# A spectral block with an MLP: evicting an item ahead of the casts of the one before

## The chip, the cores and the metric

The kernel runs on one core of a Trainium2 chip. The core has a matrix engine (TensorE, PE), a vector engine (VectorE, DVE), a scalar engine (ScalarE, ACT), a general one (GpSimd, POOL) and a queue for transfers (SyncE, SP). Each works through its own list of instructions in order and waits for the others by semaphores. Matmuls write into PSUM, here eight banks of 128 partitions x 512 float32. The metric is the device time of one launch in microseconds.

## The reference

```python
mod = (silu(c) @ w_mod).reshape(1, 6, 1, 512)        # sa, ca, ga, sb, cb, gb
h = layernorm(x) * (1 + ca) + sa                     # x: 2048 x 512
x = x + ga * irfft2(rfft2(h) * (w_r + 1j * w_i))
h = layernorm(x) * (1 + cb) + sb
x = x + gb * (mish(h @ w1 + b1) @ w2)                # w1: 512 x 1376, w2: 1376 x 512
```

The first half is a spectral filter, the second an MLP with a Mish between its two matrix products. The change concerns the MLP alone.

## The kernel before

The filter comes first and takes the first 150 us or so; its last steps overlap the first steps of the MLP. All matrix products of the MLP are made in fp32r with the operands split: `split` writes a rounded copy (the high part, a cast on ScalarE) and the remainder (the low part, a subtraction on VectorE), and three products of parts (`TERMS`) stand for one.

**Blocks and items.** The 2048 rows are worked in `NB` = 8 blocks of 256. For each block the 1376 hidden features are worked in `NT` = 6 items: item 0 has the last 96 features, items 1 to 5 have two tiles of 128. Step s of the loop (`mlp`, 48 in all) is item s % 6 of block s // 6. A step has

- `up`: TensorE multiplies w1 with the block's normalised input `h2`, one PSUM bank for a tile (tags A and D, two banks each);
- `mish`: for each tile ScalarE copies half of the bank with the bias added (L731) and VectorE adds the other half (L732); ScalarE applies the Mish (L734); VectorE makes four sums of the quarters (L744), which the multiplication of 2 x 2 blocks with seven products (Strassen's, in Winograd's form) needs;
- `high` and `low`: the casts (L754) and the remainders (L760) of the seven quarters and sums, the `acts` of the item;
- `down` of the item two steps earlier (`LAG` = 2): seven products of three matmuls each, added up in four banks (tags B and C, `out_ps`) over the block. Item 0 has six plain matmuls instead.

The w2 of an item is loaded (`load_w2`), its sums are made on GpSimd (`sum_w2`), and it is split in two parts (`split_w2`: raw and sums). Items 4 and 5 get theirs while block 0 runs.

**The next block's input.** In step 3 `norm_pair` normalises the next 256 rows on ScalarE (L141). In steps 4 and 5 `transpose_in` transposes half of the columns each, into a bank of tag A, then of tag D; `split_in` scales them (L624) and splits them into `h2` (L628, L629). `up` of the next block's item 0 reads all of `h2`.

**The result of a block.** In step 1 of the next block, after `down` of the last item, `gather` copies two banks and `chain` adds up the four results (L801 to L805). After the remainders of that step, `residual` finishes the sums, multiplies with the gate gb (L812), adds to x (L814) and stores.

**The last block.** Its items 4 and 5 are multiplied in the plain way (`down_last`: w2 unsplit into sums, loaded again by `load_w2`, split by `plain_w2`), so that most of the result can be added up before the last products; `finish` multiplies by the gate and stores the two halves one after the other.

The order on each engine is the order in which the program writes the instructions (`manual_schedule`); tile pools give buffers in rotation, and an instruction that takes a buffer waits for the last reader of its earlier content.

Of the kernel before, what the change touches and what calls it, by code (L numbers as in the profile page):

```python
# [30 lines left out]
def tile_spectral_block(ctx: ExitStack, tc: tile.TileContext, x_d, w1_d, b1_d, w2_d,  # L31
# [620 lines left out]
    def w2_space(t):  # L652
# [6 lines left out]
        if t == 4:  # L659
# [27 lines left out]
    def split_w2(t, sums):  # L687
# [23 lines left out]
    tsum = modr[:, 0:2].rearrange("p r (e d) -> p (r e) d", d=256)  # L711

    def up(g):
        b, t = divmod(g, NT)
        h = h2[b]
        ups[g] = []
        for e, f, rows in tiles(t):
            ps = bank("CD"[e] if g < 2 else "AD"[e])[:rows]
            fs = slice(f * P, f * P + rows)
            for k in range(4):  # L720
                nc.tensor.matmul(ps, w1h[:, k, fs], h[:, k], start=(k == 0), stop=False)  # L721
            for k in range(4):
                nc.tensor.matmul(ps[:, 0:256], w1l[:, k, fs], h[:, k, 0], start=False, stop=(k == 3))  # L723
            ups[g].append((e, f, ps))

    def mish(g):
        w = buf("g1")
        for e, f, ps in ups.pop(g):
            rows = ps.shape[0]
            o = w[:rows, 256 * e:256 * e + 256]  # L730
            nc.scalar.activation(o, ps[:, 256:], AF.Identity, bias=b1n[:rows, f:f + 1])  # L731
            nc.vector.tensor_tensor(o, o, ps[:, 0:256], op=ALU.add)  # L732
        o = w[:rows, 0:256 * e + 256]
        nc.scalar.activation(o, o, AF.Mish)  # L734
        parts = [(o, slice(0, 2))]
        if g >= total - 2:
            parts = [(w, slice(0, 4))]
        elif g % NT:
            u = buf("g2")
            a = w.rearrange("p (e s) -> p e s", s=P)  # L740
            v = u.rearrange("p (e s) -> p e s", s=P)
            for o, p, q, op in ((v[:, 0], a[:, 0], a[:, 2], ALU.add), (v[:, 1], v[:, 0], a[:, 1], ALU.subtract),
                                (v[:, 2], a[:, 1], a[:, 0], ALU.subtract), (v[:, 3], a[:, 3], v[:, 1], ALU.subtract)):
                nc.vector.tensor_tensor(o, p, q, op=op)  # L744
            parts = [(w[:, P:], slice(0, 3)), (u, slice(3, 7))]
        return parts

    def high(g, parts):
        hi, lo = acts[g] = [act.tile([P, 7, P], F32R, name=n) for n in ("ah", "al")]
        flat = []  # L750
        for r, c in parts:
            n = r.shape[0]
            h, l = (z[:n, c].rearrange("p e s -> p (e s)") for z in (hi, lo))
            nc.scalar.copy(h, r)  # L754
            flat.append((l, r, plain(h)))
        return flat

    def low(parts):
        for l, r, h in parts:
            nc.vector.tensor_tensor(l, r, h, op=ALU.subtract)  # L760

    def down(g):
        b, t = divmod(g, NT)
        a = acts.pop(g)
        if t == 0:
            out_ps[b] = out = [bank(n) for n in "CBBC"]
# [4 lines left out]
        out = out_ps[b]  # L771
        for n, half, e, r in END if g == total - 3 else RAW + SUM:
            o = out[n][:, 256 * half:256 * half + 256]
            own = n in (0, 3)
            last = t == 5 or (own and g == total - 3)
            for i, (p, q) in enumerate(TERMS):
                nc.tensor.matmul(o, a[p][:, e], w2[t][q][:, r], start=(own and half == 0 and t == 1 and i == 0),  # L777
                                 stop=(last and i == 2 and (n, half) != (1, 0)), skip_group_check=own)

    def down_last():  # L780
        out = out_ps[NB - 1]
        for n, half in ((2, 0), (1, 1)):
            for g in (total - 2, total - 1):
                for f in range(2):
                    for i, (p, q) in enumerate(TERMS):
                        nc.tensor.matmul(out[n], acts[g][p][:, half + 2 * f],
                                         w2["plain", g % NT][q][:, 512 * f:512 * f + 512],
                                         start=False, stop=(g == total - 1 and f == 1 and i == 2))

    rows = modr[:, 0:2]  # L790

# [7 lines left out]
    def chain(b):  # L799
        p, q = done[b]  # L800
        nc.vector.tensor_tensor(rows[:, 1], out_ps[b][1], p, op=ALU.add)  # L801
        nc.vector.tensor_tensor(q[:, 0:256], q[:, 0:256], p[:, 0:256], op=ALU.add)
        nc.vector.tensor_tensor(q[:, 256:], q[:, 256:], q[:, 0:256], op=ALU.add)
        both = q[:, 256:].unsqueeze(1).to_broadcast([P, 2, 256])
        nc.vector.tensor_tensor(rows[:, 0].rearrange("p (j d) -> p j d", j=2),  # L805
                                out_ps[b][2].rearrange("p (j d) -> p j d", j=2), both, op=ALU.add)

    def residual(b):
        p, q = done.pop(b)
        nc.vector.tensor_tensor(rows[:, 1, 256:], rows[:, 1, 256:], q[:, 0:256], op=ALU.add)  # L810
        nc.vector.tensor_tensor(rows[:, 0, 256:], rows[:, 0, 256:], p[:, 256:], op=ALU.add)
        nc.vector.tensor_tensor(rows, rows, gbr.unsqueeze(1).to_broadcast([P, 2, D]), op=ALU.mult)  # L812
        xb = x[:, 2 * b:2 * b + 2, :]
        nc.vector.tensor_tensor(xb, xb, rows, op=ALU.add)  # L814
        nc.sync.dma_start(ov[:, 2 * b:2 * b + 2, :], xb)

    total = NB * NT
    ctx.enter_context(tc.manual_schedule())

    def mlp(s):  # L820
        b, t = divmod(s, NT)
        nxt = 2 * b + 2 if b < NB - 1 else None
        up(s)
        if t in (4, 5) and nxt:
            transpose_in(nxt, t - 4)
        if t == 3 and nxt:
            norm_pair(nxt)
# [12 lines left out]
        if t == 1 and b:  # L840
            residual(b - 1)

    def finish():
        b = NB - 1
        p, q = buf("h"), buf("h")
        nc.scalar.copy(p, out_ps[b][0])
        nc.scalar.copy(q, out_ps[b][3])
        u, v = rows[:, 1], rows[:, 0]
        nc.scalar.copy(u[:, 0:256], p[:, 0:256])
        nc.vector.tensor_tensor(q[:, 0:256], q[:, 0:256], p[:, 0:256], op=ALU.add)  # L850
        nc.vector.tensor_tensor(u[:, 256:], q[:, 0:256], p[:, 256:], op=ALU.add)  # L851
        nc.vector.tensor_tensor(v[:, 0:256], q[:, 256:], q[:, 0:256], op=ALU.add)
        nc.vector.tensor_tensor(v[:, 256:], v[:, 0:256], p[:, 256:], op=ALU.add)
        nc.gpsimd.tensor_tensor(u, u, gbr, op=ALU.mult)  # L854
        down_last()
        xu, xv = x[:, 2 * b + 1, :], x[:, 2 * b, :]
        nc.vector.tensor_tensor(v, out_ps[b][2], v, op=ALU.add)
        nc.vector.tensor_tensor(v, v, gbr, op=ALU.mult)
        nc.vector.tensor_tensor(xv, xv, v, op=ALU.add)
        nc.sync.dma_start(ov[:, 2 * b:2 * b + 1, :], x[:, 2 * b:2 * b + 1, :])  # L860
        nc.gpsimd.tensor_tensor(xu, xu, u, op=ALU.add)
        nc.vector.tensor_tensor(q, out_ps[b][1], gbr, op=ALU.mult)
        nc.vector.tensor_tensor(xu, xu, q, op=ALU.add)
        nc.sync.dma_start(ov[:, 2 * b + 1:2 * b + 2, :], x[:, 2 * b + 1:2 * b + 2, :])

    apply_gate()
    prep = {s: [] for s in range(N2 + 1)}
# [32 lines left out]
        if s in (7, 8):  # L900
            split_in(0, s - 7)
    norm_scale(N2 - 4, N2)
    low(high(0, mish(0)))
    split_w2(0, False)
    low(high(1, mish(1)))
    load_w2(4)
    sum_w2(4, 0, 1, 2, 3)
    for s in range(LAG, total):
        mlp(s)
        if s == 3:  # L910
            split_w2(4, False)
            split_w2(4, True)
            load_w2(5)
            sum_w2(5, 0, 1, 2, 3)
        if s == 5:
            split_w2(5, False)
            split_w2(5, True)
        if s == total - 4:
            load_w2(4)
        if s == total - 3:  # L920
            plain_w2(4)
            load_w2(5)
        if s == total - 2:
            plain_w2(5)
    finish()


def _constants():
# [133 lines left out]
```

## Time and profile before

| | us |
|---|---|
| median of three runs | 427.79 (426.19 to 429.06) |
| the profiled execution | 427.04 |
| its span | 425.23 |
| six blocks, from the input's wait of block 1 to that of block 7 | 196.01 |
| from there to the end of the span | 42.1 |

The span is the time from the first to the last instruction of the profiled execution. The profile has a busy time for each engine, a chain of waits, and a timeline; TensorE's rows give the start of a matmul and its modelled end, so that in a dense stretch the distance of two starts is what a matmul costs, and a row in square brackets names what the engine waited for.

### The profile page before, as it was taken

The page shows a single profiled execution, that of the slowest core. Times are in us where ns is not written, and L with a number is a line of the kernel's source. Part 1 is how long each engine was busy: PE and PEld are TensorE (multiplying, and loading weights), DVE is VectorE, ACT ScalarE, POOL GpSimd, SP SyncE. Part 2 cuts the span into 40 slices and gives each one's busy share as a digit, 9 for nine tenths or more (in the row PEclk, how much of TensorE's full clock was granted, in tenths as well). Part 3 has the DMA queues.
Part 4 walks back from the last instruction along what each step waited for, and adds up shares of the span by engine and source line. Part 5 has one row for each costly group of instructions (what it writes and reads, how often), then busy time and mean ns, then how long its engine had stood idle before and what let it go on. Part 6 is the DMA issues. An engine that isn't in the chain of part 4 may idle for free.

```text
span 425.2 us, 7487 instructions
## 1 busy us (share of the span) xinstructions
PE 394.4 (93%) x2791; PEld 360.6 (85%) x2791; DVE 300.6 (71%) x654; ACT 253.3 (60%) x546; POOL 91.1 (21%) x127
## 2 busy tenths in 40 slices
PE   8999899999999999689989989989989989999994
PEld 8888788899899998588879979979979979888883
DVE  2999959676189986786766765775774774764866
ACT  2777755577459646774674674575475484475371
POOL 0677526565067521110000000000000000000002
PEclk9999999999999999899999999999999999999999
DMA  8999852281223411100100100100100100100211
GB/s 290 350 359 356 252 200 76 81 321 47 76 83 100 134 43 27 51 2 0 51 0 2 49 2 0 52 0 2 52 0 2 49 2 0 51 2 2 99 51 49
DMA packets 20180, 35.73 MB, mean 84 GB/s; under 512 B 3632, under 2 KB 6480, under 8 KB 19760
## 3 DMA queue, kind: packets, MB, share of 16 engines
q1 hardware_dynamic: 19712, 34.73, 24.0%
q10 hardware_dynamic: 432, 0.53, 0.3%
q8 instruction: 22, 0.36, 0.3%
q14 instruction: 14, 0.11, 0.1%
HBM read 31.06 MB, written 4.19 MB: 83 GB/s over the span
## 4 chain that ended last, share of the span: by engine, by line
DVE 40%; PE 25%; ACT 19%; issue 6%; DMA 5%; POOL 3%; SPq 0%; POOLq 0%; DVEq 0%; ACTq 0%
PE bank L721 6%; DVE buf L744 6%; DVE buf L732 5%; ACT buf L734 5%; DVE al L760 5%; PE bank L777 4%; DMA buf<-in_B_w_dram 4%; PE bank L723 3%; DVE st L112 3%; PE bank L456 3%; PE bank L502 3%; ACT ah L754 3%; ACT buf L141 2%; DVE ve L125 2%; ACT buf L624 2%
## 5 line engine op out<-in xcount | busy, mean ns | idle before, releaser
L760 DVE TENSOR_TENSOR al<-buf,ah 128x512 fp32r<-128x512 f32 (+2 forms) x86 | 50.1, 603 | 20.6 <-ACT ah L754 20.6
L734 ACT ACTIVATE buf<-buf 128x512 f32<-128x512 f32 (+1 forms) x48 | 28.6, 597 | 53.4 <-DVE buf L732 53.4
L744 DVE TENSOR_TENSOR buf<-buf 128x128 f32<-128x128 f32 x152 | 39.8, 303 | 28.2 <-ACT buf L734 25.8
L721 PE MATMUL bank<-h2e,w1h 128*128 128x512 f32 (+1 forms) x176 | 50.6, 407 | 8.7 <-DVE h2e L629 4.4
L754 ACT CAST ah<-buf 128x512 fp32r<-128x512 f32 (+2 forms) x86 | 45.5, 552 | 18.2 <-DVE buf L744 11.0
L721 PE MATMUL bank<-h2o,w1h 128*128 128x512 f32 (+1 forms) x176 | 49.5, 399 | 6.9 <-DVE h2o L629 5.6
L731 ACT ACTIVATE buf<-bank,b1n 128x256 f32<-128x256 f32 (+1 forms) x88 | 38.5, 467 | 28.2 <-PE bank L723 28.2
L732 DVE TENSOR_TENSOR buf<-buf,bank 128x256 f32<-128x256 f32 (+1 forms) x88 | 34.0, 416 | 26.2 <-ACT buf L731 26.2
L854 POOL TENSOR_TENSOR modr<-modr 128x512 f32<-128x512 f32 x1 | 1.3, 1343 | 234.6 <-DVE modr L851 234.6
L721 PEld LDWEIGHTS bank<-h2e,w1h 128*128 128x128 f32 (+1 forms) x176 | 30.5, 191 | 15.1 <-DVE h2e L629 5.8
L721 PEld LDWEIGHTS bank<-h2o,w1h 128*128 128x128 f32 (+1 forms) x176 | 29.8, 187 | 13.2 <-DVE h2o L629 7.4
L777 PE MATMUL bank<-w2a,ah 128*128 128x256 f32 x168 | 36.8, 285 | 0.0
L777 PE MATMUL bank<-w2b,ah 128*128 128x256 f32 x147 | 31.8, 283 | 0.0
L723 PEld LDWEIGHTS bank<-h2e,w1l 128*128 128x128 f32 (+1 forms) x176 | 27.2, 189 | 4.2
L723 PEld LDWEIGHTS bank<-h2o,w1l 128*128 128x128 f32 (+1 forms) x176 | 26.7, 185 | 4.1
L723 PE MATMUL bank<-h2e,w1l 128*128 128x256 f32 (+1 forms) x176 | 28.2, 283 | 0.0
L777 PEld LDWEIGHTS bank<-w2a,ah 128*128 128x128 f32 x168 | 28.0, 191 | 0.0
L723 PE MATMUL bank<-h2o,w1l 128*128 128x256 f32 (+1 forms) x176 | 27.8, 280 | 0.0
L234 PE MATMUL bank<-buf,mring 128*128 128x512 f32 x48 | 21.4, 446 | 4.2 <-DVE buf L227 1.9
L637 PE MATMUL bank<-kc,d 128*128 128x128 f32 x128 | 24.9, 276 | 0.5 <-ACT d L360 0.5
L112 DVE BATCH_NORM_STATS2 st<-x 128x6 f32<-128x512 f32 x32 | 22.0, 688 | 4.3 <-DMA x<-in_A_x_dram 3.9
L638 PE MATMUL bank<-kc,d 128*128 128x128 f32 x128 | 24.7, 275 | 0.0
(216 smaller groups left out, 1015.5 us busy)
## 6 DMA issues: line engine op xcount, KB each, us to landing
buf<-in_B_w_dram SPq DMA_DIRECT2D x22, 256.0 KB, 2.7
xring<-in_x_t_dram SPq DMA_DIRECT2D x16, 256.0 KB, 4.7
x<-in_A_x_dram SPq DMA_DIRECT2D x16, 256.0 KB, 5.0
wm<-in_w_mod_dram SPq DMA_DIRECT2D x16, 256.0 KB, 4.3
out_dram<-x SPq DMA_DIRECT2D x7, 512.0 KB, 2.6
mraw<-in_km_dram SPq DMA_DIRECT2D x16, 128.0 KB, 4.8
wqa<-in_w_q_dram SPq DMA_DIRECT2D x8, 256.0 KB, 4.3
wqb<-in_w_q_dram SPq DMA_DIRECT2D x8, 256.0 KB, 4.7
```

Of the source, the lines that this page charges most:

```text
L112: nc.vector.bn_stats(t, x[:, n, :])
L637: nc.tensor.matmul(o, dj[:, 0:128], kc[0][:, n, :], start=True, stop=False)
L638: nc.tensor.matmul(o, dj[:, 64:192], kc[1][:, n, :], start=False, stop=True)
L721: nc.tensor.matmul(ps, w1h[:, k, fs], h[:, k], start=(k == 0), stop=False)
L723: nc.tensor.matmul(ps[:, 0:256], w1l[:, k, fs], h[:, k, 0], start=False, stop=(k == 3))
L731: nc.scalar.activation(o, ps[:, 256:], AF.Identity, bias=b1n[:rows, f:f + 1])
L732: nc.vector.tensor_tensor(o, o, ps[:, 0:256], op=ALU.add)
L734: nc.scalar.activation(o, o, AF.Mish)
L744: nc.vector.tensor_tensor(o, p, q, op=op)
L754: nc.scalar.copy(h, r)
L760: nc.vector.tensor_tensor(l, r, h, op=ALU.subtract)
L777: nc.tensor.matmul(o, a[p][:, e], w2[t][q][:, r], start=(own and half == 0 and t == 1 and i == 0), stop=(last and i == 2 and (n, half) != ...
```

## The change

- The step is put together anew. `front` (bias and add) of item s comes first, then the casts and remainders of item s - 1 (`halves`, cast and remainder of each part in turn), then `back` (Mish and the four sums) of item s. `down` stays two steps behind. The preamble makes `front` of items 0 and 1 ahead of the first Mish.
- Both input transposes, and both of their splits, stand in step 4, the block's fifth item.
- `gather` and `chain` come after `back` in step 1, `residual` at the end of step 2 instead of step 1.
- In block 0 the raw part of the w2 of items 4 and 5 is split one step away from its sums.
- The last block has its items in the order 1, 2, 3, 4, 5, 0 (`item`). Items 3, 4, 5 and 0 are plain, go to two banks of their own and use a w2 that GpSimd has multiplied by the gate beforehand (`gate_w2`). The sums of items 1 and 2 are finished, gated and added to x while the plain items run; at the end each bank is added to x and stored.

```diff
+    def item(g):
+        b, i = divmod(g, NT)
+        return b, (i + 1) % NT if b == NB - 1 else i
+
+    def gate_w2(t):
+        for r in st["w2", t]:
+            nc.gpsimd.tensor_tensor(r, r, gbr[:r.shape[0]], op=ALU.mult)
+
     def plain_w2(t):
-        h, l = w2["plain", t] = [w.rearrange("p e d -> p (e d)") for w in w2[t - 3]]
+        h, l = w2["plain", t] = [w.rearrange("p e d -> p (e d)") for w in w2[(3, 1, 2)[t - 3]]]
...
-    def mish(g):
-        w = buf("g1")
+    def front(g):
+        st["w", g] = w = buf("g1")
         for e, f, ps in ups.pop(g):
             rows = ps.shape[0]
             o = w[:rows, 256 * e:256 * e + 256]
             nc.scalar.activation(o, ps[:, 256:], AF.Identity, bias=b1n[:rows, f:f + 1])
             nc.vector.tensor_tensor(o, o, ps[:, 0:256], op=ALU.add)
-        o = w[:rows, 0:256 * e + 256]
+
+    def back(g):
+        b, t = item(g)
+        w = st.pop(("w", g))
+        o = w if t else w[:96, 0:256]
         nc.scalar.activation(o, o, AF.Mish)
...
-    def high(g, parts):
+    def halves(g, parts):
         hi, lo = acts[g] = [act.tile([P, 7, P], F32R, name=n) for n in ("ah", "al")]
-        flat = []
         for r, c in parts:
-            n = r.shape[0]
-            h, l = (z[:n, c].rearrange("p e s -> p (e s)") for z in (hi, lo))
-            nc.scalar.copy(h, r)
-            flat.append((l, r, plain(h)))
-        return flat
-
-    def low(parts):
-        for l, r, h in parts:
-            nc.vector.tensor_tensor(l, r, h, op=ALU.subtract)
+            split(*(z[:r.shape[0], c].rearrange("p e s -> p (e s)") for z in (hi, lo)), r)
...
+    def last_down(g, t):
+        a = acts.pop(g)
+        if t == 3:
+            out_ps["last"] = bank("A"), bank("D")
+        for half in range(2):
+            o = out_ps["last"][half]
+            for f in range(2 if t else 1):
+                for i, (p, q) in enumerate(TERMS):
+                    if t:
+                        nc.tensor.matmul(o, a[p][:, half + 2 * f], w2["plain", t][q][:, 512 * f:512 * f + 512],
+                                         start=(t == 3 and f == 0 and i == 0), stop=False)
+                    else:
+                        nc.tensor.matmul(o, a[p][:96, half], w2[0][q][:96], start=False, stop=(i == 2))
...
-    def mlp(s):
-        b, t = divmod(s, NT)
+    def mlp(s, parts):
+        b, i = divmod(s, NT)
         nxt = 2 * b + 2 if b < NB - 1 else None
         up(s)
-        if t in (4, 5) and nxt:
-            transpose_in(nxt, t - 4)
-        if t == 3 and nxt:
+        if i == 4 and nxt:
+            for g in range(2):
+                transpose_in(nxt, g)
+        front(s)
+        halves(s - 1, parts)
+        parts = back(s)
+        if i == 3 and nxt:
             norm_pair(nxt)
-        parts = mish(s)
-        if t in (4, 5) and nxt:
-            split_in(nxt, t - 4)
-        if t == 1 and b:
-            down(s - LAG)
+        if i == 4 and nxt:
+            for g in range(2):
+                split_in(nxt, g)
+        down(s - LAG)
+        if i == 1 and b:
             gather(b - 1)
-        parts = high(s, parts)
-        if t != 1 or not b:
-            down(s - LAG)
-        if t == 1 and b:
             chain(b - 1)
-        low(parts)
-        if t == 1 and b:
+        if i == 2 and b:
             residual(b - 1)
-
-    def finish():
+        if s == total - 3:
+            gather(b)
+            chain(b)
+        if s == total - 2:
+            residual(b)
+        return parts
+
+    def finish(parts):
         b = NB - 1
...
+        halves(total - 1, parts)
+        down(total - 2)
+        down(total - 1)
+        for i in range(2):
+            n = 2 * b + i
+            nc.vector.tensor_tensor(x[:, n, :], x[:, n, :], out_ps["last"][i], op=ALU.add)
+            nc.sync.dma_start(ov[:, n:n + 1, :], x[:, n:n + 1, :])
...
-    low(high(0, mish(0)))
+    front(0)
+    front(1)
+    halves(0, back(0))
     split_w2(0, False)
-    low(high(1, mish(1)))
+    parts = back(1)
     load_w2(4)
     sum_w2(4, 0, 1, 2, 3)
     for s in range(LAG, total):
-        mlp(s)
+        parts = mlp(s, parts)
+        if s in (2, 3):
+            split_w2(4, s == 3)
         if s == 3:
-            split_w2(4, False)
-            split_w2(4, True)
             load_w2(5)
             sum_w2(5, 0, 1, 2, 3)
-        if s == 5:
-            split_w2(5, False)
-            split_w2(5, True)
-        if s == total - 4:
-            load_w2(4)
-        if s == total - 3:
-            plain_w2(4)
-            load_w2(5)
-        if s == total - 2:
-            plain_w2(5)
-    finish()
+        if s in (5, 6):
+            split_w2(5, s == 6)
+        if s == total - 8:
+            load_w2(0)
+            gate_w2(0)
+        if s == total - 6:
+            split_w2(0, False)
+        if total - 5 <= s < total - 2:
+            plain_w2(s - total + 8)
+        if total - 6 <= s < total - 3:
+            load_w2(s - total + 9)
+            gate_w2(s - total + 9)
+    finish(parts)
```

More of the change, by code (lines that the diff above doesn't have):

```diff
@@ L713, in up @@
     def up(g):
-        b, t = divmod(g, NT)
+        b, t = item(g)
         h = h2[b]
@@ L732, in mish @@
             nc.vector.tensor_tensor(o, o, ps[:, 0:256], op=ALU.add)
-        o = w[:rows, 0:256 * e + 256]
+    def back(g):
+        b, t = item(g)
+        w = st.pop(("w", g))
+        o = w if t else w[:96, 0:256]
         nc.scalar.activation(o, o, AF.Mish)
[L735 to L745, printed above, removed]
@@ L746, in mish @@
-        return parts
-    def high(g, parts):
+        if t == 0:
+            return [(o, slice(0, 2))]
+        if b == NB - 1 and t > 2:
+            return [(w, slice(0, 4))]
+        u = buf("g2")
+        a = w.rearrange("p (e s) -> p e s", s=P)
+        v = u.rearrange("p (e s) -> p e s", s=P)
+        for o, p, q, op in ((v[:, 0], a[:, 0], a[:, 2], ALU.add), (v[:, 1], v[:, 0], a[:, 1], ALU.subtract),
+                            (v[:, 2], a[:, 1], a[:, 0], ALU.subtract), (v[:, 3], a[:, 3], v[:, 1], ALU.subtract)):
+            nc.vector.tensor_tensor(o, p, q, op=op)
@@ L762, in down @@
     def down(g):
-        b, t = divmod(g, NT)
+        b, t = item(g)
+        if b == NB - 1 and t not in (1, 2):
+            return last_down(g, t)
         a = acts.pop(g)
+        out = out_ps.setdefault(b, None) or [bank(n) for n in "CBBC"]
+        out_ps[b] = out
         if t == 0:
-            out_ps[b] = out = [bank(n) for n in "CBBC"]
             for n, half in ((1, 1), (2, 0)):
@@ L770, in down @@
             return
-        out = out_ps[b]
-        for n, half, e, r in END if g == total - 3 else RAW + SUM:
+        last = b == NB - 1
+        end = t == (2 if last else 5)
+        for n, half, e, r in END if last and end else RAW + SUM:
             o = out[n][:, 256 * half:256 * half + 256]
-            own = n in (0, 3)
-            last = t == 5 or (own and g == total - 3)
+            own = last or n in (0, 3)
             for i, (p, q) in enumerate(TERMS):
                 nc.tensor.matmul(o, a[p][:, e], w2[t][q][:, r], start=(own and half == 0 and t == 1 and i == 0),
[L778 to L788, printed above, removed]
+                                 stop=(end and i == 2 and (n, half) != (1, 0)), skip_group_check=own)
+    def last_down(g, t):
[11 more added lines that the diff above has]
+                        nc.tensor.matmul(o, a[p][:96, half], w2[0][q][:96], start=False, stop=(i == 2))
     rows = modr[:, 0:2]
@@ L803, in chain @@
         nc.vector.tensor_tensor(q[:, 256:], q[:, 256:], q[:, 0:256], op=ALU.add)
+        if b == NB - 1:
+            nc.vector.tensor_tensor(rows[:, 0, 0:256], out_ps[b][2][:, 0:256], q[:, 256:], op=ALU.add)
+            nc.vector.tensor_tensor(rows[:, 0, 256:], q[:, 256:], p[:, 256:], op=ALU.add)
+            return
         both = q[:, 256:].unsqueeze(1).to_broadcast([P, 2, 256])
```

27 lines of the change are left out of this document (5 added, 22 removed).

## The prediction, made before the changed kernel ran

> **What bounds the kernel now.** I read the page's totals first, then the block loop in stages, then the timeline of TensorE in one block. A block is 256 rows of the MLP, the span's second half; its ends are taken at TensorE's wait for the next block's input.
>
> ```profile
> span 425.2 us, 7487 instructions
> PE 394.4 (93%) x2791; PEld 360.6 (85%) x2791; DVE 300.6 (71%) x654; ACT 253.3 (60%) x546; POOL 91.1 (21%) x127
> 252.89:285.57 32.68, 30.76 (x208) 27.90 (x208) 21.51 (x53) 19.16 (x39) 0.00 (x0) 1.00 0.04 17
> 187.09:383.10 196.01, 184.48 (x1242) 167.42 (x1242) 131.06 (x316) 116.58 (x232) 0.00 (x0) 1.00 0.04 17
> ```
>
> The stage rows give length, then busy time of PE, PEld, DVE, ACT and POOL, granted clock, DMA. The second covers six blocks: 196.01 / 6 = 32.67 us each. VectorE needs 21.5 us of a block and ScalarE 19.2, so TensorE is the bound, but not all the time. In its timeline (start, duration, line):
>
> ```profile
> 256.42 1.09 PE L721 MATMUL bank<-h2o,w1h 128*128 128x512 f32 x4
> 259.23 0.28 PE L777 MATMUL bank<-w2c,ah 128*128 128x256 f32 x1
> 261.74 1.09 PE L721 MATMUL bank<-h2o,w1h 128*128 128x512 f32 x4
> ...
> 274.06 0.60 PE L616 MATMUL bank<-ident,buf 128*128 128x128 f32 x4
> 274.41 0.48 PE L777 MATMUL bank<-w2a,ah 128*128 128x256 f32 x2
> ...
> 276.88 0.28 PE L777 MATMUL bank<-w2a,al 128*128 128x256 f32 x1
> 277.61 1.20 PE L721 MATMUL bank<-h2o,w1h 128*128 128x512 f32 x4 [0.45 <-DVE buf L732]
> ...
> 283.46 0.62 PE L721 MATMUL bank<-h2e,w1h 128*96 128x512 f32 x2
> 285.57 0.70 PE L721 MATMUL bank<-h2e,w1h 128*96 128x512 f32 x2 [1.48 <-DVE h2e L629]
> ```
>
> Starts tell what work costs: `up` of an item 259.23 - 256.42 = 2.81 us, `down` 261.74 - 259.23 = 2.51 (21 matmuls, 0.12 each), one transpose group 0.35. Two places lose time. At 277.00 (0.12 after 276.88) `up` of item 5 was due and came at 277.61: 0.61 us, for a bank that `transpose_in` had taken from the rotation. At 283.46 two matmuls of the next block go, 0.23 each, and the third, due at 283.92, comes at 285.57: 1.65 us, waiting for the second half of the next h2. So a block without waits takes 32.67 - 2.26 = 30.4 us.
>
> Why h2 is late, on ScalarE and VectorE:
>
> ```profile
> 282.60 0.63 ACT L734 ACTIVATE buf<-buf 128x512 f32<-128x512 f32 x1 [0.82 <-DVE buf L732]
> 283.13 1.00 ACT L624 ACTIVATE buf<-bank,cols 128x256 f32<-128x256 f32 x2
> 284.17 0.62 ACT L628 CAST h2e<-buf 128x512 fp32r<-128x512 f32 x1
> 284.82 0.69 DVE L629 TENSOR_TENSOR h2e<-buf,h2e 128x512 fp32r<-128x512 f32 x1 [0.54 <-ACT h2e L628]
> ```
>
> The second transpose group comes only after `up` of item 5, and its split then stands behind that item's Mish.
>
> **Part 1, both transposes in item 4 and the new step order: blocks 1 to 6.** TensorE does the same work, so the two waits are what can go; the question is what is late next. The tightest place is the store of the previous block and what follows it:
>
> ```profile
> 261.05 1.02 DVE L744 TENSOR_TENSOR buf<-buf 128x128 f32<-128x128 f32 x4 [0.70 <-ACT buf L734]
> 262.06 1.04 ACT L754 CAST ah<-buf 128x384 fp32r<-128x384 f32 x2
> 264.13 1.15 DVE L760 TENSOR_TENSOR al<-buf,ah 128x384 fp32r<-128x384 f32 x2
> 264.75 0.47 ACT L731 ACTIVATE buf<-bank,b1n 128x256 f32<-128x256 f32 x1 [0.93 <-PE bank L723]
> 265.99 1.23 DVE L812 TENSOR_TENSOR modr<-modr 128x1024 f32<-128x1024 f32 x1
> 267.25 1.23 DVE L814 TENSOR_TENSOR x<-x,modr 128x1024 f32<-128x1024 f32 x1
> 271.42 1.52 ACT L141 ACTIVATE buf<-x,nmr,rstd 128x512 f32<-128x512 f32 x2
> ```
>
> I lay the new order on these times. In item 1 nothing of `chain` moves: it ends where L760 starts, at 264.13. Item 2's second bias is ready at 265.22 (264.75 + 0.47), its add at 265.65; the casts of item 1 (1.04) end at 266.25, their lows at 266.85, the Mish at 266.9, its four adds (1.02) at 267.9. Now `residual` (0.71 for two small adds, the time from L760's end to L812; 1.26 and 1.23) ends at 271.1, item 3's adds (0.75, half of them beside its first bias) at 271.85, its Mish at 272.5, the two norms (1.52) at 274.0. TensorE reaches the transposes at 274.06: a margin of under 0.1 us, the thinnest of the block. Item 2's lows end near 273.0, and its `down` follows at 274.76. From 274.0 ScalarE does item 4's biases (two of 0.47), item 3's casts (1.04), a Mish (0.63) and two splits of 1.6 each (L624 and L628): 279.8 at the latest; VectorE's last low of h2 is 0.69 later, 280.5. TensorE is done with `down`, `up`, `down` at 274.76 + 2.51 + 2.81 + 2.51 = 282.6: 2.1 us to spare. Item 4's adds end near 275.4, ahead of `up` of item 5 at 277.3. Both waits go: 6 x 2.26 = **-13.6 us**. No engine gets more work; what costs nothing here is hidden by TensorE's 5.3 us per item.
>
> **Part 2, block 0, with the split of w2 spread over two steps.**
>
> ```profile
> 163.65 1.10 PE L721 MATMUL bank<-h2e,w1h 128*128 128x512 f32 x4
> 178.54 2.07 PE L721 MATMUL bank<-h2e,w1h 128*128 128x512 f32 x4 [2.94 <-DVE buf L732]
> 187.55 0.70 PE L721 MATMUL bank<-h2o,w1h 128*96 128x512 f32 x2 [1.11 <-DVE h2o L629]
> ...
> 176.93 1.23 DVE L685 TENSOR_TENSOR w2b<-modr,w2b 128x1024 fp32r<-128x1024 f32 x1
> 178.07 0.74 DVE L732 TENSOR_TENSOR buf<-buf,bank 128x256 f32<-128x256 f32 x2
> 179.51 2.70 DVE L744 TENSOR_TENSOR buf<-buf 128x128 f32<-128x128 f32 x4 [0.70 <-ACT buf L734]
> ...
> 178.00:182.00 4.00, 3.46 (x11) 2.94 (x12) 3.27 (x7) 2.57 (x5) 2.88 (x4) 0.57 0.28 98
> 158.95 1.28 ACT L734 ACT_TABLE_LOAD   x1
> ```
>
> From 163.65 to the third matmul of block 1 TensorE has three `up` (8.43), three `down` (7.53), two transpose groups (0.70) and two matmuls (0.46): 17.1, so 180.8; it came at 187.55, 6.8 late. The largest piece is item 4's add at 178.07, behind both splits of w2 item 4; after that idle the granted clock is 0.57 for four microseconds and the four matmuls take 2.07 instead of 1.09. With half of the split gone to item 2's step I place that add near 175.8, and TensorE is due there at 175.9. Against it: the Mish table load (1.28) now follows the biases of item 1, so `down` of item 0 starts about 0.9 later, and the four sums on GpSimd still collide with VectorE (2.70 for four adds instead of 1.02). I take **-5.5 us** (of 6.8), bounds -3.5 and -6.4.
>
> **Part 3, the last block.**
>
> ```profile
> 383.57 0.71 PE L721 MATMUL bank<-h2o,w1h 128*96 128x512 f32 x2 [1.48 <-DVE h2o L629]
> 418.54 0.61 PE L786 MATMUL bank<-w2a,ah 128*128 128x512 f32 x2
> 418.99 0.39 PE L786 MATMUL bank<-w2a,al 128*128 128x512 f32 x1
> ...
> 416.49 0.42 DVE L852 TENSOR_TENSOR modr<-buf 128x256 f32<-128x256 f32 x1
> 416.94 1.39 DVE L853 TENSOR_TENSOR modr<-modr,buf 128x256 f32<-128x256 f32 x1
> 421.46 0.69 DVE L863 TENSOR_TENSOR x<-x,buf 128x512 f32<-128x512 f32 x1
> ...
> 416.71 1.34 POOL L854 TENSOR_TENSOR modr<-modr 128x512 f32<-128x512 f32 x1 [234.65 <-DVE modr L851]
> buf<-in_B_w_dram SPq DMA_DIRECT2D x22, 256.0 KB, 2.7
> ```
>
> Before: 383.10 to 419.38 on TensorE, 36.28 us, then 5.85 to the end at 425.23. After: `up` 5 x 2.81 and half of one (1.40) for item 0, `down` 4 x 2.51, three plain items of 12 x 0.23 = 2.76 (0.45 for two, L786), and six such, 1.38, for item 0: 35.2, then one add (0.69) and the same 3.08 from the last add to the end: 3.9. Without waits that is -3.1. But seven gate multiplies on GpSimd (1.34 each), and behind them the casts and lows of three plain items instead of two, now stand on queues. A load waits for its buffer, lands 2.7 later, is gated, and the cast of it holds ScalarE's biases of the next item: by my replay 0.8 us on a bank of item 0, and 0.6 at the last lows, behind `residual` (another 3.1 of VectorE). So 1.4 at least. The upper bound: a VectorE operation beside a GpSimd one took 1.39 where its twin took 0.42 just before; if the gates hold VectorE in each item, I replay 4.2 us. I take 2.6, the middle, as neither end is nearer to these rows: **-0.5 us**, bounds -3.1 and +1.3. SP's stores and loads keep their order; the load of item 5 waits behind block 6's store, which is done first anyway.
>
> A rule bears on this: the Trainium skill, SBUF — State Buffer, "Who interferes with whom", says that a VectorE instruction with two SBUF inputs blocks wholly against a GpSimd one that reads SBUF. By that rule, the trace agrees: 1.39 against 0.42. It speaks for the upper end.
>
> **Sum.** 427.04 (the profiled execution: span 425.23 and 1.81 around it) - 13.6 - 5.5 - 0.5 = 407.4, say **407.5 us**. The profiled execution lies 0.75 under the median 427.79, within the runs' 426.19 to 429.06, so about 1% is what a measurement tells from no change.
>
> **Rivals.**
> 1. *VectorE becomes the bound at the norm.* Item 3's add, Mish and norm now stand behind `residual`. Margin under 0.1 us: each microsecond of lateness there costs 6. For it: the thin margin and my replay's error of some tenths. Against: L812 and L814 run at one duration in every block. At 1 us late: 413.5. Chance 0.14.
> 2. *The tail loses to the gates.* As by the upper bound, and a microsecond or two more where loads queue: 409.5 to 412. Chance 0.14.
> 3. *The change misses its aim at the boundary:* h2 is split no earlier because item 4's step grows by 3.2 us of splits and the wait of 1.65 only moves. Then only 6 x 0.61, 5.5 and 0.5 go: 417.5. Against it the 2.1 us to spare. Chance 0.07.
> 4. *Slower.* Products of item s now become ready one step later, and `down` reads them in the next. Place: `down` of each item; cover: from the end of `up` 2.51 + 2.81 = 5.3 against bias, casts and low, 0.47 + 1.04 + 0.69 = 2.2, so 3.1. If the engines run later than that in every item, `down` waits five times a block. It decides against me from 19.6 / 35 = 0.56 us a wait, 3.7 us of lateness; at 4.0 (0.9 a wait) 35 x 0.9 - 19.6 makes 439. Against: 21.5 and 19.2 us of work in 30.4 leave no room for such a lag to last, except in item 3. Chance 0.04.
>
> **Chances and range.** The forecast has 0.61. TensorE's own floor, 427.04 - 13.6 - 6.4 - 3.1 = 404, ends the range below, less a microsecond for the runs' scatter: 403. Above, rivals 1 and 2 with 1.4 us late at the norm: 416. Left out are rival 3, rival 4 and what of rival 1 is later still: under 2 in 10. Slower by over 1% is rival 4, 0.04; within 1% is where rivals 1 and 3 meet, 0.04 out of their 0.21; faster by over 1% is the rest, 0.92.
>
> **What would show it.** In the changed profile: a block period near 30.4 with no wait before the first `up` of a block and none before item 5's; the transposes of item 4 either unwaited or late by tenths on the norm's Mish chain; no clock dip in block 0 and no 2.9 us gap; seven GpSimd multiplies of about 1.34 in the last 45 us with VectorE operations of over 1 us beside them; two adds and two stores at the end. Wrong if the period stays over 31.5, or a wait for `ah` or `al` stands before `down` in each item.

## The result and the profile after

The changed kernel takes 409.96 us (median of four runs, 409.24 to 410.52) against 427.12 (426.19 to 429.06) beside it: a ratio of 0.959, 95% interval 0.955 to 0.963. It is 17 us faster; forecast were 407.5, range 403 to 416. The profiled execution took 410.52, its span 408.64; it is the slowest of the four, with a mean granted clock of 0.989 where the other three have 0.996.

The page's totals of the changed kernel, and three stages of it (length, then busy time of PE, PEld, DVE, ACT and POOL, granted clock, DMA share, GB/s): six blocks, one block, and the last block with the end. Line numbers have moved: L729 and L731 are `up`, L739 the bias, L740 the add, L746 the Mish, L688 and L689 cast and remainder, L782 `down`, L794 the plain items, L706 the gate on GpSimd, L828 the addition of `residual` to x.

```profile
span 408.6 us, 7462 instructions
PE 392.8 (96%) x2782; PEld 361.4 (88%) x2782; DVE 307.6 (75%) x653; ACT 249.7 (61%) x547; POOL 100.0 (24%) x132
PEclk9999999999999999999999999999999999999978
...
180.80:362.52 181.72, 181.72 (x1244) 167.68 (x1243) 133.65 (x316) 113.09 (x230) 2.68 (x2) 1.00 0.06 21
241.38:271.66 30.28, 30.28 (x209) 27.94 (x208) 21.59 (x53) 18.62 (x38) 0.00 (x0) 1.00 0.05 18
362.52:408.64 46.12, 38.75 (x216) 33.03 (x214) 32.58 (x58) 18.80 (x38) 7.76 (x5) 0.90 0.16 52
```

The six blocks take 181.72 us, 30.29 each, and TensorE is busy for the whole of it, where it had been busy for 184.48 of 196.01. What is lost stands in the last block: 46.12 us where it was 42.1, at a granted clock of 0.90.

| stage, profiled executions | before | after | change | forecast |
|---|---|---|---|---|
| up to block 1's first `up` (180.80; before it is 187.09, the late third matmul less the two ahead of it) | 187.1 | 180.8 | -6.3 | -5.5 |
| blocks 1 to 6 | 196.0 | 181.7 | -14.3 | -13.6 |
| last block and end | 42.1 | 46.1 | +4.0 | -0.5 |
| span | 425.2 | 408.6 | -16.6 | -19.6 |

The boundary in the timeline of the changed kernel (ScalarE's norm, the transposes on TensorE, the last remainder of the next h2, and its first `up`):

```profile
261.11 1.51 ACT L141 ACTIVATE buf<-x,nmr,rstd 128x512 f32<-128x512 f32 x2
262.95 1.03 PE L616 MATMUL bank<-ident,buf 128*128 128x128 f32 x8
268.25 0.69 DVE L629 TENSOR_TENSOR h2e<-buf,h2e 128x512 fp32r<-128x512 f32 x1 [0.88 <-ACT h2e L628]
271.66 1.10 PE L729 MATMUL bank<-h2e,w1h 128*96 128x512 f32 x4
```

The norms end at 262.62, 0.33 us before TensorE comes to the transposes; h2 is whole at 268.94, 2.7 us before it is read. No row of `up` in blocks 1 to 6 carries a wait.

The last block, on TensorE, ScalarE, VectorE, GpSimd and SyncE's queue:

```profile
389.83 0.39 PE L794 MATMUL bank<-w2hi,al 128*128 128x512 f32 x1
393.69 2.02 PE L729 MATMUL bank<-h2o,w1h 128*96 128x512 f32 x4 [3.48 <-DVE buf L740]
...
390.45 0.62 ACT L688 CAST w2a<-buf 128x512 fp32r<-128x512 f32 x1 [1.81 <-POOL buf L706]
391.86 0.62 ACT L688 CAST w2a<-buf 128x512 fp32r<-128x512 f32 x1 [0.79 <-POOL buf L706]
392.38 0.83 ACT L739 ACTIVATE buf<-bank,b1n 128x256 f32<-128x256 f32 x2
...
371.76 2.27 DVE L689 TENSOR_TENSOR al<-buf,ah 128x384 fp32r<-128x384 f32 x2
382.94 2.20 DVE L828 TENSOR_TENSOR x<-x,modr 128x1024 f32<-128x1024 f32 x1
385.07 1.28 DVE L689 TENSOR_TENSOR w<-buf,w 128x512 fp32r<-128x512 f32 x2
...
380.35 3.71 POOL L706 TENSOR_TENSOR buf<-buf,modr 128x512 f32<-128x512 f32 x2 [6.88 <-DVE modr L823]
389.12 2.70 POOL L706 TENSOR_TENSOR buf<-buf,modr 128x512 f32<-128x512 f32 x2 [5.06 <-DMA buf<-in_B_w_dram]
...
385.78 1.05 SPq L677 DMA_DIRECT2D buf<-in_B_w_dram  x2
391.00:401.00 10.00, 7.31 (x22) 5.72 (x23) 7.29 (x12) 4.19 (x10) 0.82 (x1) 0.66 0.00 0
```

Read backwards: the last `up` was due at 390.06 (0.23 after 389.83) and came at 393.69, 3.6 us late, for a bank whose add had to wait for biases that ScalarE gave at 392.38. ScalarE stood at the cast of item 5's w2, which waited for the gates (389.12 to 391.82), these for loads issued at 385.78, and these for a buffer that VectorE's remainder at 385.07 set free. That remainder stands behind `residual`, whose 1024-wide operations took 2.20 us beside the gates at 380.35, where they took 1.23 before. By an estimate from these rows, a `residual` of the old length would have let the second of the two remainders start about 1 us earlier and not 2: its cast waited until 384.10 for the second gate. The two gates, held in their turn, took 3.71 us where those at 389.12 took 2.70. After the wait the clock is halved: four matmuls take 2.02 us, and the granted clock is 0.66 over the ten microseconds from 391, the first 2.7 of which are still the wait.

### The profile page after: what moved, and what is told of

The parts are those of the page before. It is cut to its first block, busy times and chain, and to the rows that moved or that the text cites. A ratio compares the mean times of both kernels' runs of the same rounds, so it can differ in the third digit from the quotient of the medians.

```text
span 408.6 us, 7462 instructions
## 1 busy us (share of the span) xinstructions
PE 392.8 (96%) x2782; PEld 361.4 (88%) x2782; DVE 307.6 (75%) x653; ACT 249.7 (61%) x547; POOL 100.0 (24%) x132
## 4 chain that ended last, share of the span: by engine, by line
PE 67%; DVE 21%; ACT 5%; issue 3%; DMA 2%; POOL 1%; SPq 0%; POOLq 0%; ACTq 0%
PE bank L782 21%; PE bank L729 18%; PE bank L731 9%; DVE st L112 4%; PE bank L456 3%; PE bank L502 3%; DVE ve L125 3%; PE bank L774 2%; PE bank L794 2%; DVE x L650 2%; PE bank L489 2%; PE bank L616 1%; DVE w2a L689 1%; PE bank L435 1%; DVE buf L227 1%
## 5 line engine op out<-in xcount | busy, mean ns | idle before, releaser
L739 ACT ACTIVATE buf<-bank,b1n 128x256 f32<-128x256 f32 (+1 forms) x88 | 40.8, 470 | 67.4 <-PE bank L731 67.4
L740 DVE TENSOR_TENSOR buf<-buf,bank 128x256 f32<-128x256 f32 (+1 forms) x88 | 35.4, 416 | 41.1 <-ACT buf L739 41.1
L706 POOL TENSOR_TENSOR buf<-buf,modr 128x512 f32<-128x512 f32 (+1 forms) x7 | 10.4, 1511 | 204.8 <-DMA buf<-in_B_w_dram 197.9
L689 DVE TENSOR_TENSOR al<-buf,ah 128x512 fp32r<-128x512 f32 (+2 forms) x85 | 54.2, 659 | 4.3 <-ACT ah L688 4.3
L729 PE MATMUL bank<-h2o,w1h 128*128 128x512 f32 (+1 forms) x176 | 49.3, 402 | 3.5 <-DVE buf L740 3.5
L729 PE MATMUL bank<-h2e,w1h 128*128 128x512 f32 (+1 forms) x176 | 48.5, 397 | 0.0
L688 ACT CAST ah<-buf 128x512 fp32r<-128x512 f32 (+2 forms) x85 | 43.0, 548 | 2.6 <-PE bank L794 2.6
L756 DVE TENSOR_TENSOR buf<-buf 128x128 f32<-128x128 f32 x148 | 37.2, 293 | 3.5 <-ACT buf L746 2.2
L729 PEld LDWEIGHTS bank<-h2o,w1h 128*128 128x128 f32 (+1 forms) x176 | 30.5, 190 | 8.5 <-DVE buf L740 3.9
L746 ACT ACTIVATE buf<-buf 128x512 f32<-128x512 f32 (+1 forms) x48 | 28.6, 596 | 12.3 <-DVE buf L740 12.3
L782 PE MATMUL bank<-w2a,ah 128*128 128x256 f32 x161 | 34.9, 286 | 0.0
L729 PEld LDWEIGHTS bank<-h2e,w1h 128*128 128x128 f32 (+1 forms) x176 | 30.1, 187 | 4.5
L782 PE MATMUL bank<-w2b,ah 128*128 128x256 f32 x147 | 31.8, 283 | 0.0
L731 PEld LDWEIGHTS bank<-h2o,w1l 128*128 128x128 f32 (+1 forms) x176 | 27.1, 188 | 4.3
L731 PEld LDWEIGHTS bank<-h2e,w1l 128*128 128x128 f32 (+1 forms) x176 | 26.7, 185 | 4.2
L731 PE MATMUL bank<-h2o,w1l 128*128 128x256 f32 (+1 forms) x176 | 28.2, 283 | 0.0
L731 PE MATMUL bank<-h2e,w1l 128*128 128x256 f32 (+1 forms) x176 | 27.8, 280 | 0.0
L782 PEld LDWEIGHTS bank<-w2a,ah 128*128 128x128 f32 x161 | 26.7, 191 | 0.0
```

The costliest lines, as they stand in the source:

```text
L689: nc.vector.tensor_tensor(l, r, plain(h), op=ALU.subtract)
```

## The experiments

The theory after the result: the transposes and the step order make the loop dense, and the new last block costs 4 us because of its gates. The first four runs ask which part of the change brings what, the next three why the last block is slow, the last three test what was learnt.

**The old last block behind the new loop.**

```diff
-        return b, (i + 1) % NT if b == NB - 1 else i
+        return b, i
...   # down, down_last, finish and the loads and splits of w2 for
...   # items 4 and 5 as in the kernel before; no gate_w2, no last_down
```

> The changed kernel with the last block as it was before (items 0 to 5, items 4 and 5 plain and ungated, sums gated at the end). Theory: the loop's gain stands by itself and the new last block costs 4 us, so the block period stays 30.3 us, the last block falls from 46.1 to about 42 us, and the time is about 406.4 us, 4 less than the changed kernel. Rival (the last block's new order is part of what lets the loop run dense, or the old one runs worse behind the new step): the last block takes 44 us or more and the time is 408.5 or above.

Measured: 406.25 us (405.74 to 407.94), ratio 0.952 (0.947 to 0.957). Its two stages:

```profile
180.86:362.58 181.72, 181.72 (x1244) 167.69 (x1243) 131.79 (x316) 113.07 (x230) 0.00 (x0) 1.00 0.05 18
362.58:403.96 41.38, 35.53 (x225) 31.28 (x223) 27.73 (x59) 18.00 (x37) 2.70 (x2) 0.97 0.16 52
```

The loop is the same to the hundredth, the last block 4.7 us shorter. The theory holds: the two parts are independent, and the new last block is a loss.

**The transposes apart again, in the new step order.**

```diff
-        if i == 4 and nxt:
-            for g in range(2):
-                transpose_in(nxt, g)
+        if i in (4, 5) and nxt:
+            transpose_in(nxt, i - 4)
...
-            for g in range(2):
-                split_in(nxt, g)
+        if i in (4, 5) and nxt:
+            split_in(nxt, i - 4)
```

> The changed kernel with the transposes and their splits in items 4 and 5 again, step order new. Theory: both parts are needed at the boundary. The second split then ends about 4.4 us after item 5's up, TensorE is ready for it after 3.3, so about 1.1 us of wait before each next block, none before item 5's up; period 31.4, time near 418. Rival (the step order alone does it): no wait, period 30.3, time near 410.

Measured: 417.67 us. Six blocks took 188.42 us, 31.40 each. The boundary on TensorE:

```profile
244.22 0.62 PE L729 MATMUL bank<-h2o,w1h 128*96 128x512 f32 x2
245.74 0.69 PE L729 MATMUL bank<-h2o,w1h 128*96 128x512 f32 x2 [0.90 <-DVE h2o L629]
```

The third matmul was due at 244.68 and came 1.06 late, in every block; before item 5's `up` nothing waits. So the rest of the change, without the transposes' move, takes away the 0.6 and a third of the boundary's wait.

**The transposes together in the old kernel, nothing else.**

```diff
-        if t in (4, 5) and nxt:
-            transpose_in(nxt, t - 4)
+        if t == 4 and nxt:
+            for g in range(2):
+                transpose_in(nxt, g)
...   # split_in in the same way
```

> The kernel before with nothing but both transposes and both splits moved to item 4. Theory: the wait of 1.65 us at the boundary goes, the one before item 5's up shrinks to about 0.2, period about 30.5 us in place of 32.67; block 0 keeps its gap, so the time is near 427 - 13 = 414. Rival (the old step order can't carry both splits in one step): a wait of over 1 us stays in each block, period 31.5 or more, time over 420.

Measured: 412.54 us (411.92 and 413.17), ratio 0.965 (0.960 to 0.971). The six blocks, the last four of them, block 1's wait at the transposes, and block 0's gap:

```profile
183.74:368.02 184.28, 183.62 (x1244) 167.93 (x1243) 131.12 (x316) 117.03 (x232) 0.00 (x0) 1.00 0.05 18
245.92:368.02 122.10, 122.10 (x830) 112.01 (x829) 86.01 (x209) 77.12 (x153) 0.00 (x0) 1.00 0.05 18
...
206.17 1.09 PE L616 MATMUL bank<-ident,buf 128*128 128x128 f32 x8 [0.47 <-DVE buf L732]
178.31 1.21 PE L721 MATMUL bank<-h2e,w1h 128*128 128x512 f32 x4 [2.49 <-DVE buf L732]
```

184.28 / 6 = 30.71 us a block: this one edit brings 1.96 of the 2.38 us per block. From block 3 on it is 122.10 / 4 = 30.53 with no wait left; block 1 still waits 0.47 us at the transposes and 0.19 at item 5's `up`. The edit brings more than was expected of it in all, 14.4 in place of 13, because block 0 gains 3.35 too (its boundary comes at 183.74 in place of 187.09) though its gap stays: at 2.49 us of idling, against 2.94 in the kernel before, the four matmuls behind it take 1.21 us and not 2.07.

**Both halves of w2's split in one step of block 0.**

```diff
-        if s in (2, 3):
-            split_w2(4, s == 3)
         if s == 3:
+            split_w2(4, False)
+            split_w2(4, True)
...   # the same for item 5 after step 5
```

> The changed kernel with both halves of the split of w2 in one step again (after item 3 and after item 5 of block 0). Theory: item 4's add in block 0 stands behind both halves again and a wait of about 1 to 2 us comes back before item 5's up of block 0; the time is 1 to 3 us above the changed kernel, the later period unchanged. Rival (the new step order alone removes block 0's gap): no wait there, block 1 starts at 181 as in the changed kernel.

Measured: 410.98 us, one run. Block 1 starts at 182.64, 1.84 us later than in the changed kernel, which looks like the theory; but no wait stands before item 5's `up`, and ScalarE's last statistics of the filter already end later. From the ScalarE row at 157.62 in the changed kernel, and from its counterpart at 159.45 here, to block 1 (the changed kernel first):

```profile
157.62:180.80 23.18, 22.26 (x147) 20.05 (x146) 19.48 (x47) 20.62 (x43) 6.17 (x7) 1.00 0.13 36
```

```profile
159.45:182.64 23.19, 21.48 (x142) 19.32 (x142) 19.88 (x46) 20.67 (x43) 5.95 (x7) 1.00 0.11 36
```

23.18 and 23.19: by this one run the spread is worth nothing in the new step order. The expectation fell. The 1.8 us lie in the filter, which no edit touches; the runs show block 1 at 180.8 to 182.9, so stages are compared from there on.

**The last block without gates.**

```diff
     def gate_w2(t):
-        for r in st["w2", t]:
-            nc.gpsimd.tensor_tensor(r, r, gbr[:r.shape[0]], op=ALU.mult)
+        return
```

> The changed kernel without the seven gate multiplies on GpSimd (the last block's plain items then leave out the gate; all else is done). Theory: the gates are a part of the last block's loss, by the time they add between a load and its cast and by the VectorE operations that they hold (1024-wide ones 2.20 us in place of 1.23). Item 5's casts then come about 2 us earlier, the 3.6 us wait before the last up shrinks to 1.5 to 2, the clock stays full, and the last block takes 46.1 - 2 - 3 = about 41 us; time near 405.5. Rival (the loads alone, which wait for their buffers, hold the queue): the wait stays above 3 us, the last block above 45 us.

Measured: 405.54 us. The last block, the second 1024-wide operation of `residual` in it, and the last `up`:

```profile
364.36:403.23 38.87, 35.24 (x216) 31.07 (x214) 27.92 (x58) 18.93 (x38) 0.00 (x0) 1.00 0.18 62
...
382.76 1.22 DVE L827 TENSOR_TENSOR x<-x,modr 128x1024 f32<-128x1024 f32 x1
391.19 1.09 PE L728 MATMUL bank<-h2o,w1h 128*96 128x512 f32 x4
```

7.25 us less than with gates, more than the 5 expected. No wait is left on TensorE, VectorE's row is back at 1.22, and the clock is full, though the loads still wait for the same buffers. The gates are the loss, not the loads by themselves.

The run before this one (both halves of w2's split in one step) has the gates, and its last block begins at the same 364.36:

```profile
364.36:409.20 44.84, 37.50 (x216) 32.13 (x214) 32.52 (x58) 18.80 (x38) 7.97 (x5) 0.96 0.16 54
395.47 1.68 PE L729 MATMUL bank<-h2o,w1h 128*96 128x512 f32 x4 [3.40 <-DVE buf L740]
```

So by this pair the gates cost 44.84 - 38.87 = 5.97 us, less than the 7.25. Of these, the last `up` comes 4.28 later (395.47 against 391.19), and 3.00 of that were there when item 5's loads were issued (387.61 against 384.61): that is as much as VectorE lost, about 1.0 on the remainders beside the first gate and on each of the two 1024-wide operations. The other 1.3 came between the loads and the last `up`, where the gates stand between a load and its cast. What is left lies behind the last `up`, most of it the clock.

**Loads and gates earlier.**

```diff
-        if total - 6 <= s < total - 3:
-            load_w2(s - total + 9)
-            gate_w2(s - total + 9)
+        for t, tag, at in ((3, "y", 6), (4, "t", 6), (5, "y", 5)):
+            if s == total - at:
+                load_w2(t, tag)
+                gate_w2(t)
...   # load_w2 takes the buffers of that tag
```

> The changed kernel with the loads and gates of the plain items earlier: item 4's w2 goes into the two buffers of the input splits, which the last block doesn't use, and is loaded together with item 3's; item 5's is loaded one step earlier, ahead of block 6's store on SyncE's queue. Theory: what is late in the last block is the data of the casts that stand ahead of the last items' biases on ScalarE. With the data there in time no wait stands before the last up, the clock stays full, the last block takes 39.5 to 40.5 us, and the time is 403.5 to 405, under the old last block's 406.25. Rival (GpSimd holding VectorE is the cost, whenever the gates run): the wait moves to another place of the last block, which stays at 43 us or more; time 408 or above.

Measured: 409.87 us (409.07 to 410.22); the last block takes 43.90 us. VectorE, three rows of TensorE, and GpSimd:

```profile
375.93 3.09 DVE L756 TENSOR_TENSOR buf<-buf 128x128 f32<-128x128 f32 x4
386.99 2.19 DVE L828 TENSOR_TENSOR x<-x,modr 128x1024 f32<-128x1024 f32 x1
...
379.67 0.50 PE L782 MATMUL bank<-w,ah 128*128 128x256 f32 x2 [1.21 <-DVE modr L810]
381.19 0.50 PE L782 MATMUL bank<-w,ah 128*128 128x256 f32 x2 [0.90 <-DVE modr L818]
383.79 1.91 PE L729 MATMUL bank<-h2o,w1h 128*128 128x512 f32 x4
...
374.01 4.45 POOL L706 TENSOR_TENSOR buf<-buf,modr 128x512 f32<-128x512 f32 x3 [14.16 <-DMA buf<-in_B_w_dram]
384.33 3.78 POOL L706 TENSOR_TENSOR buf<-buf,modr 128x512 f32<-128x512 f32 x2 [5.86 <-DMA buf<-in_B_w_dram]
```

The theory fell and its rival held. The wait before the last `up` is down to 0.66 us, but three gates in a row now stand beside the four sums of an item, which take 3.09 us in place of 1.02. `chain` follows them on VectorE, and `down` waits for it, 1.21 and 0.90 us, with an `up` at half rate behind these waits (1.91 us for four matmuls). In both places where the gates were tried, VectorE pays.

**The wait filled with matmuls that add nothing.**

```diff
+        if t == 3:
+            for i in range(12):
+                nc.tensor.matmul(o, zero, w2["plain", 3][0][:, 0:512], start=False, stop=False)
...   # zero is a 128 x 128 tile of zeros, made on VectorE ahead of the MLP
```

> The changed kernel with 12 matmuls more, of a zero matrix, after the down of item 3 in the last block: 2.8 us of work that adds nothing, in the wait before the last up. Theory: the halved clock behind that wait is a cost by itself, of about 3 us; with the wait filled to under 1 us the clock stays full, the wait ends at the same time, and the last block takes about 43 us, time near 407.5. Rival (the clock falls for another reason, or costs nothing since the engines behind are late anyway): the rows stay at half rate or the last block stays at 45 to 46 us.

Measured: 409.96 us, its last block 43.47 us. The filling and the last `up`:

```profile
392.21 2.88 PE L802 MATMUL bank<-w2hi,zero 128*128 128x512 f32 x12
395.80 1.17 PE L731 MATMUL bank<-h2o,w1h 128*96 128x512 f32 x4 [0.71 <-DVE buf L742]
```

The four matmuls take 1.17 us in place of 2.02, and the block is 2.65 us shorter, though the last `up` comes as late after the block's start (395.80 - 364.64 = 31.16 us) as in the changed kernel (393.69 - 362.52 = 31.17): that is what the halved clock cost behind one long wait in the changed kernel's profiled execution. It doesn't always cost as much. Three other runs have the same last block and the same wait (3.39 to 3.42 us): the transposes apart, both halves of the split in one step, and the longer store at the end of this section. From the last `up` to the end of the span they take 13.41, 13.73 and 14.66 us, the changed kernel 14.95, the filled wait 12.3. So the halved clock costs between 1.1 and 2.65 us. What sets how long it lasts, the runs don't show. The time is no better than the changed kernel's median: block 1 began 2.1 us later here, and by their mean clock the executions around the median had lost less than the profiled one.

**The gate after the sum.**

```diff
-            nc.vector.tensor_tensor(x[:, n, :], x[:, n, :], out_ps["last"][i], op=ALU.add)
+            q = buf("h")
+            nc.vector.tensor_tensor(q, out_ps["last"][i], gbr, op=ALU.mult)
+            nc.vector.tensor_tensor(x[:, n, :], x[:, n, :], q, op=ALU.add)
...   # and no gate on w2
```

> The changed kernel with the gate where the plain sums end: no gate on w2, and at the end each of the two banks is multiplied by the gate into a buffer (0.69 us on VectorE) and the product added to x (0.69). Theory: the last block without the GpSimd gates took 38.9 us; the two multiplies add 1.0 to 1.4 behind the last matmul, so about 40.1 us, against 41.4 with the old last block: 1.3 us under that one, time 404.8 to 406 on the same chip. Rival (the gain without gates was the missing work at the end of the chain, not the engines beside it): 42 us or more, slower than the old last block.

Measured: 405.40 us (404.87 to 405.56), ratio 0.950 (0.947 to 0.952); the last block 40.19 us. Two multiplies at the end cost 1.3 us where seven on GpSimd cost 6.0 to 7.25.

**The old last block again, on the same chip.** The kernel of the first experiment.

> The kernel with the old last block once more, beside the one that gates after the sum, on the same chip. Theory: 406.3 us again, last block 41.4 us, 1.3 us above the kernel that gates after the sum. Rival: the two can't be told apart, or this one is the faster.

Measured: 406.18 us (405.44 to 407.36), ratio 0.952 (0.949 to 0.955), last block 41.12. The gate after the sum is 0.8 us ahead of it by the medians and 0.9 by the last blocks, but the intervals overlap: the two can't be told apart. Both beat the changed kernel by 4 us.

**A longer store.**

```diff
+        if b < NB - 2:
+            nc.vector.tensor_tensor(rows, rows, rows, op=ALU.add)
```

> The changed kernel with one more 128x1024 addition on VectorE (1.22 us, its result isn't used) behind the store of each of the blocks 0 to 5. Theory: the norm's place has the thinnest margin, 0.33 us in the changed profile, and what is late there is paid in full by TensorE at the transposes: 0.9 us in each of six blocks, period 31.2 us, 5.4 us in all, time near 415.5. Rival (the queues take it up): period 30.3 us, time near 410.

Measured: 416.35 us; six blocks take 187.30 us, 31.22 each. The transposes, and the norm on ScalarE:

```profile
265.72 0.33 PE L616 MATMUL bank<-ident,buf 128*128 128x128 f32 x1
266.42 0.77 PE L616 MATMUL bank<-ident,buf 128*128 128x128 f32 x5 [0.37 <-ACT buf L141]
...
264.87 1.50 ACT L141 ACTIVATE buf<-x,nmr,rstd 128x512 f32<-128x512 f32 x2
```

0.93 us a block for 1.22 us of VectorE work, where 0.9 was expected: all but the margin of 0.33 is paid by TensorE. The margin is as thin as the timeline says.

## Why the prediction was right

**What bounds it** was right: TensorE with two waits per block. The two waits, read at 0.61 and 1.65 us, are gone in every block.

**Part 1** was right in mechanism and 0.7 us short in size: 30.29 us a block, not 30.4. The difference is that a wait costs a little beyond itself: the four matmuls behind the bank wait took 1.20 us in the row that the prediction shows (277.61), and 1.09 where nothing waited (256.42), which is 0.11 and about the 0.13 (the pair behind the boundary's wait, 0.70 against 0.62, would add 0.08, so the sum isn't exact). The replay of the tightest place gave the norms' end 0.06 us before TensorE needs them; it was 0.33. I had laid rows end to end by their length, but on VectorE and on ScalarE the next row starts a little before the end, as here the four sums and what follows them in the changed kernel:

```profile
255.68 1.01 DVE L756 TENSOR_TENSOR buf<-buf 128x128 f32<-128x128 f32 x4
256.61 0.41 DVE L823 TENSOR_TENSOR modr<-modr,buf 128x256 f32<-128x256 f32 x1
```

0.93 us from start to start for a row of 1.01; a few such steps in a row make up the 0.27. That rival 1 was real, though not met, is shown by the longer store. How the gain divides was not forecast: the transposes' move alone gives 1.96 of 2.38 us, the rest of the change without it 1.27.

**Part 2**: -6.3 against -5.5, inside the bounds. 0.4 of it lie ahead of the change (the filter's statistics end at 157.62 in place of 158.04), so the part itself gave 5.9. The size isn't firm: the same filter ended 1.8 us later, at 159.45, in another run. And the reason was in part wrong: the spread of w2's split, which I put first, brings nothing in the one run that tests it. From the same row of the filter to block 1 it is 29.05 us before, 25.60 with the transposes moved and nothing else, and 23.18 with the whole change; so 3.4 of the 5.9 come with the transposes, the rest with the new step order, which brings item 4's add in time with the split in either place.

**Part 3** is the term that failed: -0.5 forecast, +4.0 measured, beyond its upper bound of +1.3, and so are the 44.84 and 45.77 us of two other runs with this last block (+2.7 and +3.6). The count of the work was right: 3.1 less without waits makes 39.0, and the kernel without gates took 38.87. (Small slips stand in that sum: 0.69 and 3.08 make 3.8, the middle of 1.4 and 4.2 is 2.8, and 4.2 leads to +1.1; they change 0.2 us.) What failed is the 2.6 us for waits, which were 6.0 to 7.25. The wait of the last `up` was in the replay, at 0.8 us without collisions; it was 3.6. The step that went wrong is "the upper bound": in that replay, of which the prediction prints only the 4.2 us, I let the gates hold VectorE for the length of one operation an item, while `residual`, two 1024-wide operations in a row, lost 2 us to them after the remainders had lost 1, and VectorE passed these 3 us on to the buffers, the loads and ScalarE's queue. And I left out the clock: in block 0 I had read that it falls to half after a long idle, but did not ask whether the last block would make a new one. It did, and that cost 2.65 us in the profiled execution, 1.1 to 2.4 in three others. Rival 2 named the mechanism and sized it at 2 to 4.5 us above the forecast; the last block alone came out 4.5 above, and the 1.5 us gained elsewhere beyond the forecast brought the profiled execution to 410.5. So the total came within 3 us of the forecast in part because two errors offset each other. By the rule of the Trainium skill, SBUF — State Buffer, "Who interferes with whom", that speaks for the upper end, the runs agree: the same operation took 2.20 us with GpSimd reading SBUF and 1.22 without.

**Rivals 3 and 4** did not come: the boundary has 2.7 us to spare, and no `down` waits for its products.

## What to carry to other kernels

When TensorE is dense but for one wait per block, follow the wait to the operation that is late and ask which engine's queue it stands in: here two splits taken out of the queue behind the last item's Mish gave most of the gain. An idle engine isn't free: seven multiplies on a GpSimd that had nothing to do cost 6 to 7 us, 3 of them by holding VectorE, and two on VectorE at the end cost 1.3. Size the end of a kernel by laying each queue out, a wait's effect on the clock included; there is nothing behind it to absorb an error.

## What the runs showed of the hardware

- A TensorE wait of 2.94 us (block 0 before) or of 3.48 (last block after) was followed by matmuls at half rate (a granted clock of 0.57 from 178 to 182 and 0.66 from 391 to 401), one of 2.49 (only the transposes moved) was not. With the loads earlier the rows were at half rate again behind two shorter waits, 1.21 and 0.90, so the length of one wait doesn't decide it; what does stays open. Behind four waits of 3.39 to 3.48 the price was 1.1, 1.4, 2.4 and 2.65 us. With matmuls of a zero matrix in the wait the rows behind it were at full rate (1.17 us for four, against 2.02).
- A 128x1024 VectorE operation between SBUF tiles took 2.20 us beside GpSimd multiplies, and 1.22 without them; the multiplies were lengthened too, two in 3.71 us where two others took 2.70.
